# Making the next tile's input over six steps of the second part, with its product on GpSimd

## The chip, the cores and the metric

The kernel runs on one core of a Trainium2 chip. The metric is the device time of one execution in microseconds (us); the time before is the median of 3 runs. A TensorE matmul needs its weights loaded first (PEld in the profile), and the load of the next weights runs beside the matmul before it.

## The reference

Two things follow each other. First a long convolution by Fourier transforms, multiplied by the input; then a feed-forward layer on the result:

```python
h_filt = (np.maximum(pos_emb @ w1, 0.0) @ w2) * window      # 12480 x 128
u = x * v                                                   # 2 x 12480 x 128
y = irfft(rfft(u, 2 * S) * rfft(h_filt, 2 * S))[:, :S, :]
a = (x * y).reshape(24960, 128)
h = a @ w_in                                                # 128 -> 2048
return (h * (1.0 / (1.0 + np.exp(-h)))) @ w_out             # 2048 -> 128
```

All arrays are float32.

## The kernel before

The transform is written as matmuls in stages (98 x 64 points), with the spectrum in pairs of frequencies. The program has a first part, in which the filter and the transform of batch 0 are made, and a second part, the loop over `steps` (L886), which is the feed-forward layer with the transform of batch 1 beside it.

The second part goes over 52 token tiles of up to 490 columns (tokens), and in each over 16 blocks f of 128 hidden values; one (tile n, block f) is a step s. A tile's input is a pair ah, al: the high part of a = x * y, rounded to the type that TensorE takes, and the rest. A step does

- three matmuls into hq, a PSUM tile with three buffers: high weights with ah (L893), high weights with al (L894), low weights with ah (L895);
- Silu on ScalarE (L900), into hq itself while work of batch 1 is left (`beside`), otherwise into the SBUF tile g with two buffers;
- the rounding of the result to gh, on VectorE (L902), or on ScalarE (L904) when f is a multiple of 4 (of 5 once nothing is beside);
- the low part gl on VectorE (L905), which reads the Silu result and gh;
- three matmuls of the step three before (LAG) into op (L921 to L923), the output's sum.

Every engine takes its instructions in the order in which they stand in the program. There are no other priorities. Between the steps `batch1_steps` (a generator, L777) puts the work of batch 1, spread evenly over the first 384 steps: first groups of stage A (product x * v on GpSimd L269, matmuls L238, copies L244), then, for each of 49 pairs of frequencies, loads of tables (L315) and of the filter's spectrum (L795) on SP's queue, roundings on ScalarE (L803), low parts on GpSimd (L809), matmuls L441, products and sums on VectorE and GpSimd (L466, L473, L479, L483), and a store.

The input of the next tile is made by `attn_tile` (L668), all of it behind step f = 8 (L907): 80 small matmuls into yp (L677), a copy of half of yp to s2 on ScalarE (L688), the sum and the difference on VectorE (L691, L692, and for some tiles one column more, L699), the product with x on VectorE (L702), the rounding to ah on ScalarE (L703), the rest al on VectorE (L704). For tile 0 the same function is called ahead of the loop (letter Y of the hand-written order `seq3`, L746). The data for the tile after the next come by `load_tile` (L656) behind step f = 9: two requests on SP's queue, one for the transform's output of all tokens of the tile (L660), one for x (L665). Each has one buffer, so the first waits until the matmuls L677 have read it and the second until L702 has.

Of the kernel before, what the change touches and what calls it, by code (L numbers as in the profile page):

```python
# [14 lines left out]
ALU = mybir.AluOpType  # L15
# [44 lines left out]
def tile_offsets():  # L60
    offs, o = [], 0
    for b, i, t2, n in token_tiles():
        offs.append(o)
        o += sum(tile_widths(i, n))
    return offs, o
# [21 lines left out]
def kernel(  # L87
# [17 lines left out]
    nc = tc.nc  # L105
    ctx.enter_context(tc.manual_schedule())

    def pool(name, **kw):
        kw.setdefault("bufs", 1)
        return tc.alloc_tile_pool(name=name, reuse_waits="tile", **kw)  # L110
# [273 lines left out]
    for t in P["seq"]:  # L384
# [21 lines left out]
        elif t == "p":  # L406
            g = len(pts)
            pts.append(ppool.tile([128, NP, R], F32, name=f"pt{g}", tag="pt", bufs=8))
            for o in range(0, NP, 4) if g == 0 else [0]:
                n = 4 if g == 0 else NP  # L410
# [141 lines left out]
    def pair_u0(q):  # L552
        up = pp.tile([128, 2, NI, D], F32, name=f"up0_{q}", tag="up", bufs=2)
        for c in range(2):
            for k in range(2):
                nc.tensor.matmul(  # L556
                    up[64 * k : 64 * k + 64, c].rearrange("p i d -> p (i d)"),
                    fbs[q][:, 0, k, 64 * c : 64 * c + 64],
                    X[:, 2 * q + k],
                    start=True,  # L560
                    stop=True,
                )
        us = rp.tile([128, 2, NI, D], F32, name=f"us{q}", tag="uw", bufs=2)
        nc.scalar.copy(out=us, in_=up)  # L564
        return up, us
# [55 lines left out]
    pp = pool("pp2", space=PSUM)  # L621
# [3 lines left out]
    for it in range(-1, NQ):  # L625
        if it + 4 < NQ:
            fbs[it + 4] = load_fb(rpa, it + 4, 8, nc.sync if it < 0 else nc.scalar, fc)
        if it >= 0:
            up, us = pair_u0(it)
# [6 lines left out]
        if it >= 0:  # L636
            hab = habs.pop(it)
            at = products(it, up, hab[:, 1:2], "at", 4, nc.vector)
# [14 lines left out]
    tiles = token_tiles()  # L653
    offs, _ = tile_offsets()
# [13 lines left out]
    def attn_tile(n, wt, xs, psp, tag):  # L668
        b, i, t2, m = tiles[n]
        ws = tile_widths(i, m)  # L670
        w = sum(ws)

        yp = psp.tile([128, 2, 256], F32, name=f"yp{n}", tag=tag[0], bufs=tag[1])
        for t in range(m):
            for c in range(2):
                for h in range(0, D, 32):
                    nc.tensor.matmul(  # L677
                        yp[h : h + 32, c, t * HT : (t + 1) * HT],
                        wt[:, c, t * D + h : t * D + h + 32],
                        fai_sb[:, c],  # L680
                        start=True,
                        stop=True,
                    )
        at = mt.tile([128, 490], F32, name=f"att{n}", tag="att", bufs=1)
        ah = mt.tile([128, 512], F32R, name=f"ah{n}", tag="ah", bufs=2)
        al = mt.tile([128, 512], F32R, name=f"al{n}", tag="al", bufs=2)
        s2 = mt.tile([128, 256], F32, name=f"s2{n}", tag="s2", bufs=1)
        nc.scalar.copy(out=s2[:, 0 : m * HT], in_=yp[:, 1, 0 : m * HT])  # L688
        y1, y2 = (a[:, 0 : m * HT].rearrange("p (t j) -> p t j", t=m) for a in (yp[:, 0], s2))
        o, r = m * HT, ws[0] - HT  # L690
        nc.vector.tensor_tensor(out=at[:, 0:o].rearrange("p (t j) -> p t j", t=m), in0=y1, in1=y2, op=ALU.add)  # L691
        nc.vector.tensor_tensor(  # L692
            out=at[:, o : o + m * r].rearrange("p (t j) -> p t j", t=m),
            in0=y1[:, :, 1 : 1 + r],
            in1=y2[:, :, 1 : 1 + r],
            op=ALU.subtract,
        )
        if w > o + m * r:
            nc.vector.tensor_tensor(  # L699
                out=at[:, w - 1 : w], in0=y1[:, m - 1, HT - 2 : HT - 1], in1=y2[:, m - 1, HT - 2 : HT - 1], op=ALU.subtract  # L700
            )
        nc.vector.tensor_tensor(out=at[:, 0:w], in0=at[:, 0:w], in1=xs[:, 0:w], op=ALU.mult)  # L702
        nc.scalar.copy(out=ah[:, 0:w], in_=at[:, 0:w])  # L703
        nc.vector.tensor_tensor(out=al[:, 0:w], in0=at[:, 0:w], in1=ah[:, 0:w].bitcast(F32), op=ALU.subtract)  # L704
        return ah, al

    ahead, attn = {}, {}
    n_a = n_t = n_h = n_l = 0
    n_r = 4
    for t in P["seq3"]:  # L710
        if t == "x":
            uv.load()
        elif t in "md":
            uv.mul(nc.vector if t == "d" else nc.gpsimd)
        elif t in "Aa":
            stage_a_group(1, n_a, psa, uss.pop(n_a), 2, t == "A")
            n_a += 1
        elif t == "s":
            pair_s(*prods[NQ - 1])
        elif t == "v":  # L720
            pair_v(prods[NQ - 1][0], nc.vector)
        elif t == "u":
            last_w(NQ - 2)
        elif t == "U":
            last_w(NQ - 1)
            rp.release()
            rpa.release()
            mw = pool("mw")
            wo_split[:] = (mw.tile([128, NF * D], F32R, name=f"wo{k}") for k in "hl")
            mt = pool("mt")  # L730
        elif t == "S":
            nc.scalar.activation(out=warm_sb, in_=w2_sb[0:1, 0:1], func=AF.Silu)
        elif t == "L":
            ahead[n_t] = load_tile(n_t)
            n_t += 1
        elif t == "r":
            load_raw(n_r, spare[:, (n_r - 4) // 2 * 2, 256 * (n_r % 2) : 256 * (n_r % 2) + 256], wod)
            n_r += 1
        elif t == "h":
            split_hi(n_h, wo_split)  # L740
            n_h += 1
        elif t == "l":
            split_lo(n_l, wo_split)
            n_l += 1
        elif t == "Y":
            attn[0] = attn_tile(0, *ahead.pop(0), pp, ("up", 2))  # L746
    NA = n_a
    woh, wol = wo_split
    wih, wil = wi_split
# [7 lines left out]
    pmy = pool("pmy", space=PSUM)  # L757
# [4 lines left out]
    class Carved:  # L762


        at = dict(hab=(0,), at=(1024,), bt=(1792,), uw=(2560,), ws=(3072,), fb=(3584, 5868))
# [119 lines left out]
    op = {}  # L885
    for s in range(len(steps) + LAG):  # L886
        if s < len(steps):
            n, f = steps[s]
            w = sum(tile_widths(*tiles[n][1::2]))
            ah, al = attn[n]  # L890
            hp = pm.tile([128, 512], F32, name=f"hq{s}", tag="hq", bufs=3)
            fs = slice(f * 128, (f + 1) * 128)
            nc.tensor.matmul(hp[:, 0:w], wih[:, fs], ah[:, 0:w], start=True, stop=False)  # L893
            nc.tensor.matmul(hp[:, 0:w], wih[:, fs], al[:, 0:w], start=False, stop=False)  # L894
            nc.tensor.matmul(hp[:, 0:w], wil[:, fs], ah[:, 0:w], start=False, stop=True)  # L895
            beside = done < total
            g = hp if beside else moe.tile([128, 490], F32, name=f"g{s}", tag="g", bufs=2)
            gh = moe.tile([128, 512], F32R, name=f"gh{s}", tag="gh", bufs=P['lag'] + 1)
            gl = moe.tile([128, 512], F32R, name=f"gl{s}", tag="gl", bufs=P['lag'] + 1)
            nc.scalar.activation(out=g[:, 0:w], in_=hp[:, 0:w], func=AF.Silu)  # L900
            if f % P['fp'] if beside else f % P['fg']:
                nc.vector.tensor_copy(gh[:, 0:w], g[:, 0:w])  # L902
            else:
                nc.scalar.copy(out=gh[:, 0:w], in_=g[:, 0:w])  # L904
            nc.vector.tensor_tensor(out=gl[:, 0:w], in0=g[:, 0:w], in1=gh[:, 0:w].bitcast(F32), op=ALU.subtract)  # L905
            gs[s] = gh, gl
            if f == 8 and n + 1 < len(tiles):  # L907
                attn[n + 1] = attn_tile(n + 1, *ahead.pop(n + 1), pmy, ("yp", 1))
            if f == 9 and n + 2 < len(tiles):
                ahead[n + 2] = load_tile(n + 2)  # L910
            while done < total and done * n_side < (s + 1) * total:
                done += next(side, total)
        if s >= LAG:
            n, f = steps[s - LAG]
            w = sum(tile_widths(*tiles[n][1::2]))
            if f == 0:
                op[n] = pm.tile([128, 512], F32, name=f"op{n}", tag="op", bufs=2)
            o = op[n]
            fs = slice(f * 128, (f + 1) * 128)
            gh, gl = gs.pop(s - LAG)  # L920
            nc.tensor.matmul(o[:, 0:w], woh[:, fs], gh[:, 0:w], start=(f == 0), stop=False)  # L921
            nc.tensor.matmul(o[:, 0:w], woh[:, fs], gl[:, 0:w], start=False, stop=False)  # L922
            nc.tensor.matmul(o[:, 0:w], wol[:, fs], gh[:, 0:w], start=False, stop=(f == NF - 1))  # L923
            if f == NF - 1:
                ot = moe.tile([128, 490], F32, name=f"ot{n}", tag="ot", bufs=2)
                nc.scalar.copy(out=ot[:, 0:w], in_=o[:, 0:w])
                nc.scalar.dma_start(out=out[:, offs[n] : offs[n] + w], in_=ot[:, 0:w])
                del op[n], attn[n]
# [98 lines left out]
```

## Time and profile before

| | us |
|---|---|
| median of 3 runs (1582.66 to 1583.68) | 1583.28 |
| the profiled execution | 1582.48 |
| its span, first to last instruction | 1580.7 |

| engine | busy, us | share of the span |
|---|---|---|
| TensorE matmuls | 1536.4 | 97% |
| TensorE weight loads | 1302.8 | 82% |
| VectorE | 1273.2 | 81% |
| ScalarE | 1029.0 | 65% |
| GpSimd | 547.9 | 35% |

The mean granted TensorE clock is 0.992. Durations in the profile overlap a little: an engine starts its next instruction before the last one's end, and the ends of matmuls are modelled. An idle time is put down to the instruction whose completion came last before it ended.

### The profile page before, as it was taken

To read this page: it belongs to the slowest core of one execution; us is meant where nothing else is said; L and a number is where in the kernel's file an instruction comes from. 1 tells how busy PE (TensorE), PEld (TensorE's weight loads), DVE (VectorE), ACT (ScalarE), POOL (GpSimd) and SP (SyncE) were. 2 spreads that over 40 slices of the span, in tenths; PEclk is the share of its full clock that TensorE was granted. 3 is DMA by queue.
4 is the path that set the end of the run, shared out by engine and by line. 5 is a ranking of instruction groups with operands and counts; after the bars stand their busy time and mean duration, and the time that the engine had idled before them with its cause. 6 is when DMAs were issued, how large, how long until landed. Compare 5 with 4: busy or idle time off the path is not lost.

```text
span 1580.7 us, 34674 instructions
## 1 busy us (share of the span) xinstructions
PE 1536.4 (97%) x13420; PEld 1302.8 (82%) x13420; DVE 1273.2 (81%) x2148; ACT 1029.0 (65%) x2022; POOL 547.9 (35%) x520
## 2 busy tenths in 40 slices
PE   8979999799999999999999999999999999999999
PEld 7966776688888888888888888888888898888888
DVE  7658998666699889999999998777777777777776
ACT  2446676677777778777778775555555555555555
POOL 2557777422266656666666650000000000000000
PEclk9989999899999999999999999999999999999999
DMA  8567787734245454544554431111111111111110
GB/s 248 185 201 214 245 267 235 219 100 140 79 128 144 125 146 135 151 133 137 139 145 138 133 113 54 48 48 52 33 47 50 48 45 39 45 52 50 34 44 16
DMA packets 135213, 182.12 MB, mean 115 GB/s; under 512 B 10357, under 2 KB 78521, under 8 KB 135049
## 3 DMA queue, kind: packets, MB, share of 16 engines
q1 hardware_dynamic: 94024, 140.18, 31.1%
q10 hardware_dynamic: 40384, 37.63, 7.7%
q8 instruction: 106, 1.74, 0.5%
q0 software_dynamic: 640, 2.10, 0.4%
q14 instruction: 59, 0.48, 0.1%
HBM read 126.44 MB, written 53.42 MB: 114 GB/s over the span
## 4 chain that ended last, share of the span: by engine, by line
PE 75%; DVE 9%; ACT 4%; issue 4%; DMA 3%; POOL 2%; SPq 1%; ACTq 0%; DVEq 0%; POOLq 0%
PE hq L893 10%; PE op L921 10%; PE hq L894 10%; PE hq L895 10%; PE op L923 10%; PE op L922 10%; PE yp L677 2%; PE ap L238 2%; PE wp L609 2%; PE up L556 2%; PE ap L211 2%; DVE gl L905 2%; PE sp L573 2%; PE up L441 1%; PE wp L441 1%
## 5 line engine op out<-in xcount | busy, mean ns | idle before, releaser
L900 ACT ACTIVATE g<-hq 128x486 f32<-128x486 f32 (+3 forms) x448 | 252.8, 570 | 195.5 <-PE hq L895 175.1
L905 DVE TENSOR_TENSOR gl<-g,gh 128x486 fp32r<-128x486 f32 (+3 forms) x448 | 292.1, 657 | 73.1 <-PE hq L895 38.3
L893 PE MATMUL hq<-ah,wih 128*128 128x490 f32 (+3 forms) x832 | 320.8, 386 | 5.9 <-DVE gl L905 5.6
L921 PE MATMUL op<-gh,woh 128*128 128x490 f32 (+3 forms) x832 | 323.6, 389 | 0.0
L894 PE MATMUL hq<-al,wih 128*128 128x490 f32 (+3 forms) x832 | 317.2, 381 | 0.2 <-DVE al L704 0.2
L895 PE MATMUL hq<-ah,wil 128*128 128x490 f32 (+3 forms) x832 | 317.1, 381 | 0.0
L923 PE MATMUL op<-gh,wol 128*128 128x490 f32 (+3 forms) x832 | 316.9, 381 | 0.0
L922 PE MATMUL op<-gl,woh 128*128 128x490 f32 (+3 forms) x832 | 315.1, 379 | 0.0
L905 DVE TENSOR_TENSOR gl<-hq,gh 128x490 fp32r<-128x490 f32 (+2 forms) x384 | 250.8, 661 | 26.4 <-ACT gh L904 16.2
L900 ACT ACTIVATE hq<-hq 128x490 f32<-128x490 f32 (+2 forms) x384 | 212.4, 558 | 74.3 <-PE hq L895 46.0
L902 DVE CAST gh<-hq 128x490 fp32r<-128x490 f32 (+2 forms) x288 | 188.7, 655 | 41.4 <-ACT hq L900 39.6
L893 PEld LDWEIGHTS hq<-ah,wih 128*128 128x128 f32 x832 | 156.6, 188 | 40.8 <-DVE gl L905 16.0
L894 PEld LDWEIGHTS hq<-al,wih 128*128 128x128 f32 x832 | 158.2, 190 | 25.4 <-DVE al L704 0.7
L895 PEld LDWEIGHTS hq<-ah,wil 128*128 128x128 f32 x832 | 157.2, 189 | 24.8
L923 PEld LDWEIGHTS op<-gh,wol 128*128 128x128 f32 x832 | 156.7, 188 | 25.4
L902 DVE CAST gh<-g 128x486 fp32r<-128x486 f32 (+3 forms) x336 | 137.3, 409 | 49.9 <-ACT g L900 43.6
L921 PEld LDWEIGHTS op<-gh,woh 128*128 128x128 f32 x832 | 156.3, 188 | 23.2
L922 PEld LDWEIGHTS op<-gl,woh 128*128 128x128 f32 x832 | 156.8, 188 | 21.6 <-DVE gl L905 0.3
L703 ACT CAST ah<-att 128x490 fp32r<-128x490 f32 (+3 forms) x52 | 30.9, 595 | 97.4 <-DVE att L702 97.4
L591 POOL TENSOR_TENSOR bt<-us,hab 128x512 f32<-128x512 f32 x49 | 67.7, 1382 | 50.9 <-ACT us L564 33.3
L466 POOL TENSOR_TENSOR slots<-slots 128x512 f32<-128x512 f32 x49 | 63.5, 1296 | 61.4 <-ACT slots L460 61.4
L479 DVE TENSOR_TENSOR at<-at,bt 128x768 f32<-128x768 f32 x49 | 72.7, 1485 | 13.5 <-POOL bt L597 13.5
(1068 smaller groups left out, 2415.2 us busy)
## 6 DMA issues: line engine op xcount, KB each, us to landing
slots<-hs SPq DMA_DIRECT2D x98, 256.0 KB
slots<-wd SPq DMA_DIRECT2D x48, 490.0 KB
hs<-hab SPq DMA_DIRECT2D x49, 256.0 KB
slots<-in_fb_dram SPq DMA_DIRECT2D x49, 256.0 KB
wd<-slots ACTq DMA_DIRECT2D x49, 256.0 KB
wd<-ws SPq DMA_DIRECT2D x23, 512.0 KB
fb<-in_fc_dram ACTq DMA_DIRECT2D x45, 256.0 KB
xs<-in_x_dram SPq DMA_DIRECT2D x32, 196.0 KB
```

The costliest lines, as they stand in the source:

```text
L466: e.tensor_tensor(out=t[:, 0:2].rearrange("p k (i d) -> p k i d", i=NI), in0=u, in1=hab[:, :, m, 0].unsqueeze(2).broadcast_to([128, 2, NI, ...
L479: nc.vector.tensor_tensor(out=at, in0=at, in1=bt, op=ALU.add)
L591: e.tensor_tensor(out=t[:, 0:2].rearrange("p c (i d) -> p c i d", i=NI), in0=u, in1=h0.unsqueeze(2).broadcast_to([128, 2, NI, D]), op=ALU. ...
L893: nc.tensor.matmul(hp[:, 0:w], wih[:, fs], ah[:, 0:w], start=True, stop=False)
L894: nc.tensor.matmul(hp[:, 0:w], wih[:, fs], al[:, 0:w], start=False, stop=False)
L895: nc.tensor.matmul(hp[:, 0:w], wil[:, fs], ah[:, 0:w], start=False, stop=True)
L900: nc.scalar.activation(out=g[:, 0:w], in_=hp[:, 0:w], func=AF.Silu)
L902: nc.vector.tensor_copy(gh[:, 0:w], g[:, 0:w])
L905: nc.vector.tensor_tensor(out=gl[:, 0:w], in0=g[:, 0:w], in1=gh[:, 0:w].bitcast(F32), op=ALU.subtract)
L921: nc.tensor.matmul(o[:, 0:w], woh[:, fs], gh[:, 0:w], start=(f == 0), stop=False)
L922: nc.tensor.matmul(o[:, 0:w], woh[:, fs], gl[:, 0:w], start=False, stop=False)
L923: nc.tensor.matmul(o[:, 0:w], wol[:, fs], gh[:, 0:w], start=False, stop=(f == NF - 1))
```

## The change

`attn_tile` becomes a generator with five yields. At f = 8 it is created and run to its first yield (the matmuls and the allocation of the tiles); at each of f = 9 to 13 its next segment is issued: the copy to s2; the sum and the difference; the product, now on GpSimd; the rounding to ah; the low part al. The load for tile n + 2 moves from f = 9 to f = 12. Tile 0's input is made in one go as before, with its product on GpSimd too.

```diff
         s2 = mt.tile([128, 256], F32, name=f"s2{n}", tag="s2", bufs=1)
+        attn[n] = ah, al
+        yield
         nc.scalar.copy(out=s2[:, 0 : m * HT], in_=yp[:, 1, 0 : m * HT])
...
+        yield
         nc.vector.tensor_tensor(out=at[:, 0:o].rearrange("p (t j) -> p t j", t=m), in0=y1, in1=y2, op=ALU.add)
...
-        nc.vector.tensor_tensor(out=at[:, 0:w], in0=at[:, 0:w], in1=xs[:, 0:w], op=ALU.mult)
+        yield
+        nc.gpsimd.tensor_tensor(out=at[:, 0:w], in0=at[:, 0:w], in1=xs[:, 0:w], op=ALU.mult)
+        yield
         nc.scalar.copy(out=ah[:, 0:w], in_=at[:, 0:w])
+        yield
         nc.vector.tensor_tensor(out=al[:, 0:w], in0=at[:, 0:w], in1=ah[:, 0:w].bitcast(F32), op=ALU.subtract)
-        return ah, al
...
-            attn[0] = attn_tile(0, *ahead.pop(0), pp, ("up", 2))
+            for _ in attn_tile(0, *ahead.pop(0), pp, ("up", 2)):
+                pass
...
             if f == 8 and n + 1 < len(tiles):
-                attn[n + 1] = attn_tile(n + 1, *ahead.pop(n + 1), pmy, ("yp", 1))
-            if f == 9 and n + 2 < len(tiles):
+                nxt = attn_tile(n + 1, *ahead.pop(n + 1), pmy, ("yp", 1))
+            if 8 <= f < 14 and n + 1 < len(tiles):
+                next(nxt, None)
+            if f == 12 and n + 2 < len(tiles):
                 ahead[n + 2] = load_tile(n + 2)
```

## Rows read from the trace of the kernel before

**Rows 1.** The page, part 1: busy us, share of the span, instructions.

```profile
PE 1536.4 (97%) x13420; PEld 1302.8 (82%) x13420; DVE 1273.2 (81%) x2148; ACT 1029.0 (65%) x2022; POOL 547.9 (35%) x520
```

**Rows 2.** Three windows of the second part: busy us (instructions), clock, DMA share, GB/s.

```profile
303.35:402.79 99.44, 96.61 (x688) 84.27 (x687) 63.36 (x103) 75.36 (x150) 29.87 (x24) 0.98 0.41 122
402.79:934.26 531.47, 525.08 (x4114) 449.31 (x4113) 478.00 (x795) 408.99 (x817) 325.75 (x339) 1.00 0.49 135
934.26:1580.70 646.44, 642.63 (x4999) 548.96 (x4997) 498.17 (x943) 373.46 (x673) 5.69 (x6) 1.00 0.15 44
```

**Rows 3.** Waits, 402.79 to 934.26 us: total us, times, longest us.

```profile
ACT ah L703 <- DVE att L702: 41.5, 20, 3.1
...
PEld hq L893 <- DVE gl L905: 16.0, 31, 1.3
...
DVE al L704 <- ACT ah L703: 13.3, 20, 0.7
```

**Rows 4.** Timeline, one tile's input (yp at 579.9): start us, us, instruction, [idle before].

```profile
582.57 0.67 DVE L702 TENSOR_TENSOR att<-att,slots 128x490 f32<-128x490 f32 x1
...
583.27 0.60 ACT L703 CAST ah<-att 128x490 fp32r<-128x490 f32 x1 [1.81 <-DVE att L702]
...
586.80 0.67 DVE L905 TENSOR_TENSOR gl<-hq,gh 128x490 fp32r<-128x490 f32 x1
...
587.52 0.19 PEld L893 LDWEIGHTS hq<-ah,wih 128*128 128x128 f32 x1 [1.34 <-DVE gl L905]
...
587.86 0.39 PE L894 MATMUL hq<-al,wih 128*128 128x490 f32 x1
```

**Rows 5.** Timeline, one of the first three tiles, ScalarE and TensorE.

```profile
356.28 0.60 ACT L703 CAST ah<-att 128x490 fp32r<-128x490 f32 x1 [1.81 <-DVE att L702]
...
358.84 1.57 PE L238 MATMUL ap<-fa_sb,slots 98*128 98x196 f32 x8 [0.62 <-issue]
```

**Rows 6.** Lines, GpSimd's products: count, busy us, mean ns, idle us before them.

```profile
L466 POOL TENSOR_TENSOR slots<-slots 128x512 f32<-128x512 f32 x49 | 63.5, 1296 | 61.4 <-ACT slots L460 61.4
...
L473 POOL TENSOR_TENSOR slots<-slots 128x256 f32<-128x256 f32 x49 | 36.3, 742 | 0.0
```

**Rows 7.** Timeline, the first weight load of the second part.

```profile
303.35 0.28 PEld L893 LDWEIGHTS hq<-ah,wih 128*128 128x128 f32 x1 [0.24 <-ACT ah L703]
```

**Rows 8.** Timeline in the second half, matmuls, ScalarE and VectorE around one tile's input.

```profile
1088.79 0.58 ACT L900 ACTIVATE g<-hq 128x490 f32<-128x490 f32 x1 [0.76 <-PE hq L895]
...
1090.04 0.67 DVE L905 TENSOR_TENSOR gl<-g,gh 128x490 fp32r<-128x490 f32 x1 [0.85 <-PE hq L895]
...
1101.89 0.67 DVE L905 TENSOR_TENSOR gl<-g,gh 128x490 fp32r<-128x490 f32 x1
...
1103.23 0.67 DVE L702 TENSOR_TENSOR att<-att,slots 128x490 f32<-128x490 f32 x1
...
1104.25 0.38 PE L895 MATMUL hq<-ah,wil 128*128 128x490 f32 x1
...
1107.43 0.67 DVE L905 TENSOR_TENSOR gl<-g,gh 128x490 fp32r<-128x490 f32 x1
...
1108.46 0.67 DVE L905 TENSOR_TENSOR gl<-g,gh 128x490 fp32r<-128x490 f32 x1
...
1112.04 0.39 PE L894 MATMUL hq<-al,wih 128*128 128x490 f32 x1
```

**Rows 9.** Timeline in the first part, GpSimd's and VectorE's instructions on SBUF operands.

```profile
199.60 1.27 POOL L591 TENSOR_TENSOR bt<-us,hab 128x512 f32<-128x512 f32 x1
...
199.62 2.07 DVE L479 TENSOR_TENSOR at<-at,bt 128x768 f32<-128x768 f32 x1 [0.62 <-POOL bt L597]
...
202.87 0.95 DVE L479 TENSOR_TENSOR at<-at,bt 128x768 f32<-128x768 f32 x1
...
211.65 0.92 POOL L597 TENSOR_TENSOR bt<-us,hab 128x256 f32<-128x256 f32 x1
...
211.91 0.95 DVE L512 TENSOR_TENSOR wil<-spare,wih 128x256 fp32r<-128x256 f32 x1
```

## The prediction

> **What bounds the kernel now.** I read the shares of the engines first: TensorE is busy 97% of the span [rows 1], so a gain can only come out of the places where it stands still, and a loss out of a new such place. Next come the windows by stage [rows 2]. The second part of the program (52 tiles of 16 steps) begins at 303.35 us. Until 402.79 it runs beside the end of batch 1's first stage, until 934.26 beside batch 1's pairs (both "the first half" below), then alone ("the second half"). The reader is to see that VectorE is at 478.0 of 531.5 us in the middle window, 90%, while GpSimd is at 61% there and all but idle afterwards. TensorE's busy figures hide short stalls, so the third view is who waited for whom in the middle window [rows 3]: TensorE's weight load of a step's first matmul, L893, stood 16.0 us in 31 waits for VectorE's low part, L905. In that stretch a step's PSUM buffer hq (three of them) is only free when L905 of three steps before has read it.
>
> Fourth, one such place in order of time [rows 4]. Matmul yp of the next tile has run at 579.9. VectorE does the sum, the difference and the product L702, then stands for ScalarE's ah (13.3 us in 20 waits [rows 3]), then does al (L704). The low part of the step behind them starts only at 586.80, and the weight load that needs it at 587.52, after 1.34 us idle. ScalarE had itself stood 1.81 us for L702. So one burst on two engines, once a tile, is what TensorE pays for. In the second half the waits of TensorE are gone: a tile is 22.6 us of matmuls end to end, and the change can only lose there.
>
> The profiled execution took 1582.48 us (span 1580.7); the median of the runs is 1583.28, 0.8 higher. Terms below are differences from the profile, and are taken off the median.
>
> **The change part by part.** The generator adds no instruction. The same work for tile n+1, all issued behind step 8 before, is issued behind step 8 (matmuls), 9 (copy s2), 10 (sum, difference), 11 (product), 12 (ah) and 13 (al). It is needed at step 16, the next tile's first.
>
> 1. *The burst goes.* Lost time per wait is less than the idle time shown: in [rows 4] the load idled 1.34 up to 587.52. Loads of 0.19 us come every 0.22 when nothing is late, so this one was due at 586.21, its matmul at 586.43 and the next, L894, at 586.66. That one ran at 587.86, 1.20 late, so 0.14 of each wait is no loss. 31 waits: 16.0 - 31 x 0.14 = 11.7 us. **-11.7** if nothing new comes.
>
> 2. *In the first three tiles* the same wait of ScalarE (1.81 us) delays the copies of stage A's output, and TensorE stands 0.62 us at L238 [rows 5]. At 3 tiles about **-2.0**.
>
> 3. *The product moves.* VectorE loses 0.67 us a tile [rows 4]. GpSimd took 1296 ns for 512 columns and 742 for 256 of the same operation [rows 6], 2.16 ns a column, so 490 columns are 1.25 us (estimate). For the very first tile, which is still made in one go ahead of the loop, this lies on the path: TensorE waits for ah at 303.35 [rows 7]. 1.25 - 0.67 = **+0.6**.
>
> 4. *The product in GpSimd's queue, first half.* Behind it stand the pairs' low parts and products; ahead of it at most two operations of up to 1.3 us. GpSimd is busy 61% [rows 2] and an operation in progress has about 0.6 us left, so the product waits 0.4 us on average. ScalarE reaches ah two steps after the sum, behind Silu and, at step 12, a rounding as well; I reckon some 0.7 us of margin before al is late for step 16. One tile in four overruns, by about 0.6 us: 20 x 0.25 x 0.6 = **+3**. Bounds: 0, and 11.7 (the stall only moves to steps 13 to 16). I take a value near the lower end because GpSimd stands idle 39% of that stretch.
>
> 5. *The second half.* Here Silu's result lies in SBUF, so VectorE's L905 reads two SBUF operands, and that meets GpSimd. [Rows 9] show it: the add L479, 0.95 us alone, lasts 2.07 when it is issued 0.02 after a GpSimd product, and ends 0.82 after that product's end; so it stands until GpSimd is through. They take turns: L597 of GpSimd (211.65) gets in between two such adds of VectorE, and the second, issued at 211.91, takes 0.95 us for 256 columns. I follow one tile on its clock [rows 8]. Step 10's last hq matmul ends at 1104.63, Silu starts 0.04 later, and the low part 1.25 after Silu, as in another step whose rounding is on ScalarE (1088.79 to 1090.04): 1105.92. Low part, sum and difference take 1.34 (1101.89 to 1103.23): done at 1107.2. Product 1107.3 to 1108.55. L905 of step 11 stands behind it and ends at 1108.55 + 0.67 - 0.13 = 1109.1. Two more pairs of rounding and low part at 1.03 (1107.43 to 1108.46) and al start at 1111.1, end 1111.8; with 0.15 for the weight load 1111.9. The matmul that needs al, step 16's second, ran at 1112.04. So it just fits: 0 a tile, or up to 0.2 where the odd column's extra subtraction (0.15) comes in. 27 tiles x 0 to 0.15: **+2**.
>
> By the Trainium skill (SBUF - State Buffer, "Who interferes with whom") a cast can also run in a mode that holds the port shared with GpSimd; the cast L902 of step 11 would then hold the product up by some 0.2 us, and the term of the second half would be 4 instead of 2. No run here shows that, since GpSimd never worked beside that cast.
>
> 6. *The load of tile n+2* moves from step 9 to step 12 on SP's queue, both requests. 490 and 243 KB at the stretch's 135 GB/s [rows 2] are 5.4 us; due is the first at the next step 8, twelve steps of at least 1.33 us on. 0. The second request now waits for GpSimd's product instead of L702, and the pairs' loads of later steps queue behind it; loads of steps 9 to 11 now go ahead of it. 0, with up to 1 us in a few tiles if it fails; it is inside term 4's bounds. The buffers yp, s2 and att are held two to five steps longer and are free ten steps before their next use: 0.
>
> 7. *s2 a step later* finds its matmuls done; same length: 0.
>
> Sum: -11.7 - 2.0 + 0.6 + 3 + 2 = -8.1. 1583.3 - 8.1 = **1575.2 us**, 0.5% faster. Terms 1 to 3 alone give -13.1 (1570.2).
>
> **The rivals.** *Slower: al is late in every tile of the second half.* Place: the chain of term 5, which has 0.1 us to spare. If GpSimd gets the port only after L905 of step 11 as well, the product starts 0.7 us later, ScalarE's ah and Silu of step 13 with it, and al ends near 1112.5: 0.6 to 0.8 a tile, 27 tiles, +16 to +22. With -10.1 from the other terms that is 1589 to 1595. It decides from (10.1 + 3.2) / 27 = 0.49 us a tile. For it: VectorE is loaded without a break behind step 10, and TensorE has no slack. Against it: the turns taken in [rows 9].
>
> *No change: the stall moves.* Instead of VectorE's burst, ScalarE stands at ah for GpSimd, as it stood for L702 (41.5 us in 20 waits [rows 3]), Silu of step 13 comes late and step 16 pays; or the second half costs 0.3 a tile. Term 4 at 8 or term 5 at 8 brings the sum to about -2: 1581.5 us. For it: GpSimd is in order and its operations themselves wait for ScalarE. Against: GpSimd's slack.
>
> *The change doesn't do what it says* is excluded by the code: the operations are the same and every segment is run by step 13.
>
> **How the numbers follow.** Forecast (sum between -13 and -3.2) 0.62; no change 0.20; slower 0.18. About 0.2%, 3.2 us, is what a measurement can tell from none. The range leaves out little below (all of terms 1 and 2, nothing given back, 1569) and the worse half of the slower case above (1589).
>
> **What would show it.** Right: L893's waits for L905 fall from 16.0 us to under 5; ScalarE's wait at ah is for GpSimd and below 1 us a tile; in the second half one L905 a tile lasts 1.2 us or more, and tiles there stay within 0.2 of 22.6 us. Wrong: a wait of L894 for al in most tiles of the second half (the slower rival), or L893's waits as long as before, only later in the tile (no change).

## The result and the profile after

The changed kernel took **1604.64 us** (median of 4 runs, 1602.20 to 1607.72) beside 1582.97 for the kernel before on the same chip: a ratio of 1.0142, 95% interval 1.0127 to 1.0157. It is slower by some 22 us; the forecast was 1575.2, with a range that ended at 1589. The profiled execution took 1604.58 us, its span is 1602.7. Lines behind the edit have other numbers than before: L706 is the product, L708 ah, L710 al, L809 the pairs' roundings, L815 their low parts, L899 to L901 the hq matmuls, L906 Silu, L911 the low part gl.

First the page's part 1, against [rows 1]:

```profile
PE 1546.1 (96%) x13420; PEld 1301.8 (81%) x13420; DVE 1266.4 (79%) x2096; ACT 1033.2 (64%) x2022; POOL 623.5 (39%) x572
```

The 52 products have gone from VectorE to GpSimd, as the instruction counts say (2148 to 2096, 520 to 572). Then the same three stretches as in [rows 2]. Their cuts are the first weight loads of steps 0, 48 and 368, that is, of tiles 0, 3 and 23:

```profile
301.62:405.91 104.29, 97.87 (x687) 85.34 (x688) 61.00 (x98) 75.66 (x150) 34.32 (x27) 0.97 0.37 115
405.91:954.11 548.20, 531.52 (x4114) 449.35 (x4112) 476.81 (x775) 412.21 (x816) 361.59 (x359) 1.00 0.47 129
954.11:1602.70 648.59, 644.42 (x4999) 546.94 (x4997) 494.92 (x917) 374.42 (x674) 42.11 (x35) 1.00 0.16 45
```

The second part begins 1.73 us earlier, the first three tiles are 4.85 us longer (99.44 before), the middle stretch 16.73 (531.47 before), the second half 2.15 (646.44 before). So the loss lies where the transform of batch 1 runs beside. The cuts are not quite the ends of batch 1's stages, as the prediction takes them: in the kernel before, the first stage's last matmuls L238 end at 421.08 us and the pairs' last L441 at 949.90, so the second half begins with one more tile beside the pairs. Waits in the middle stretch (total us, times, longest), of GpSimd, TensorE's weight loads and ScalarE:

```profile
POOL att L706 <- DVE att L695: 25.4, 8, 4.2
POOL att L706 <- DVE att L702: 24.2, 10, 4.5
POOL att L706 <- ACT hq L906: 20.0, 1, 20.0
PEld hq L899 <- DVE gl L911: 11.3, 28, 1.1
...
PEld hq L900 <- DVE al L710: 8.7, 10, 1.4
...
ACT ah L708 <- POOL att L706: 2.6, 5, 1.0
...
PEld up L441 <- POOL xs15l L815: 1.6, 1, 1.6
...
PEld up L441 <- POOL xs25l L815: 1.5, 1, 1.5
```

Three readings. ScalarE's stand at ah is gone (2.6 us in 5, against 41.5 in 20 [rows 3]), as intended. But GpSimd now stands at the product for VectorE's difference: the idle times in front of the 20 products of this stretch, the one of 20.0 left out, have a mean of 2.7 us. (That one lies ahead of the pairs' first matmuls.) And TensorE waits for what was hardly ever late before: al, and the pairs' low parts on GpSimd (L441). One tile shows how these hang together (timeline of after, the step that issues the product and those behind it; start us, us, instruction, [idle before]):

```profile
693.07 0.62 ACT L809 CAST xs25h<-X 128x512 fp32r<-128x512 f32 x1
...
698.40 0.15 DVE L702 TENSOR_TENSOR att<-yp,s 128x1 f32<-128x1 f32 x1
...
698.62 1.89 POOL L706 TENSOR_TENSOR att<-att,slots 128x486 f32<-128x486 f32 x1 [4.48 <-DVE att L702]
...
700.47 1.30 POOL L815 TENSOR_TENSOR xs25l<-X,xs25h 128x512 fp32r<-128x512 f32 x1
...
701.83 0.19 PEld L441 LDWEIGHTS up<-xs25l,fw25h 128*128 128x128 f32 x1 [1.49 <-POOL xs25l L815]
...
702.40 0.75 POOL L483 TENSOR_TENSOR slots<-slots 128x256 f32<-128x256 f32 x1
...
703.18 0.62 ACT L809 CAST vs24h<-slots 128x512 fp32r<-128x512 f32 x1 [2.03 <-POOL slots L483]
...
703.71 0.56 ACT L906 ACTIVATE hq<-hq 128x486 f32<-128x486 f32 x1
...
704.30 0.66 DVE L908 CAST gh<-hq 128x486 fp32r<-128x486 f32 x1 [3.04 <-ACT hq L906]
...
705.55 1.28 POOL L466 TENSOR_TENSOR slots<-slots 128x512 f32<-128x512 f32 x1 [0.38 <-ACT slots L460]
705.58 1.78 DVE L710 TENSOR_TENSOR al<-att,ah 128x486 fp32r<-128x486 f32 x1
...
707.41 0.19 PEld L900 LDWEIGHTS hq<-al,wih 128*128 128x128 f32 x1 [1.05 <-DVE al L710]
```

The rounded xs25h was ready at 693.69. Its low part stood behind the product in GpSimd's queue until 700.47, nearly seven microseconds, and GpSimd did nothing for 4.48 of them. TensorE paid 1.49. The rest of the row comes late in turn: L483 on GpSimd, for which ScalarE stood 2.03 at the rounding vs24h, with Silu behind it, for which VectorE stood 3.04; then al, which TensorE waited for again.

In the first three tiles the product stands ahead of stage A's product x * v (L269) in the same way (timeline of after; the idle time is put down to L244, but VectorE's difference L695 had ended only at 361.96):

```profile
361.56 0.40 DVE L695 TENSOR_TENSOR att<-yp,s 128x240 f32<-128x240 f32 x1
...
362.10 1.23 POOL L706 TENSOR_TENSOR att<-att,slots 128x490 f32<-128x490 f32 x1 [15.90 <-ACT X L244]
...
363.28 2.49 POOL L269 TENSOR_TENSOR slots<-slots 98x512 f32<-98x512 f32 x2
...
364.61 1.59 PE L238 MATMUL ap<-fa_sb,slots 98*128 98x196 f32 x8 [1.89 <-POOL slots L269]
```

### The profile page after: what moved, and what is told of

Its sections match the earlier page's. It is cut to its first block, busy times and chain, and to the rows that moved or that the text cites. A ratio compares the mean times of both kernels' runs of the same rounds, so it can differ in the third digit from the quotient of the medians.

```text
span 1602.7 us, 34725 instructions
## 1 busy us (share of the span) xinstructions
PE 1546.1 (96%) x13420; PEld 1301.8 (81%) x13420; DVE 1266.4 (79%) x2096; ACT 1033.2 (64%) x2022; POOL 623.5 (39%) x572
## 4 chain that ended last, share of the span: by engine, by line
PE 55%; issue 5%; POOL 5%; DVE 4%; ACT 3%; DMA 0%; ACTq 0%; POOLq 0%; SPq 0%; DVEq 0%
PE op L929 9%; PE hq L900 9%; PE hq L899 8%; PE hq L901 8%; PE op L931 8%; PE op L930 8%; PE yp L677 2%; PE up L441 1%; DVE gl L911 1%; PE wp L441 1%; DVE al L710 1%; POOL slots L466 1%; DVE gh L908 1%; ACT hq L906 1%; POOL slots L483 1%
## 5 line engine op out<-in xcount | busy, mean ns | idle before, releaser
L906 ACT ACTIVATE g<-hq 128x486 f32<-128x486 f32 (+3 forms) x448 | 255.8, 571 | 233.3 <-PE hq L901 177.5
L911 DVE TENSOR_TENSOR gl<-g,gh 128x486 fp32r<-128x486 f32 (+3 forms) x448 | 316.6, 711 | 76.9 <-PE hq L901 41.6
L706 POOL TENSOR_TENSOR att<-att,slots 128x490 f32<-128x490 f32 (+3 forms) x52 | 66.9, 1287 | 699.2 <-DVE att L695 345.8
L899 PE MATMUL hq<-ah,wih 128*128 128x490 f32 (+3 forms) x832 | 321.4, 386 | 4.9 <-DVE gl L911 3.5
L900 PE MATMUL hq<-al,wih 128*128 128x490 f32 (+3 forms) x832 | 319.4, 384 | 6.5 <-DVE al L710 6.4
L901 PE MATMUL hq<-ah,wil 128*128 128x490 f32 (+3 forms) x832 | 316.9, 381 | 0.0
L906 ACT ACTIVATE hq<-hq 128x490 f32<-128x490 f32 (+2 forms) x384 | 213.5, 558 | 105.4 <-PE hq L901 79.5
L911 DVE TENSOR_TENSOR gl<-hq,gh 128x490 fp32r<-128x490 f32 (+2 forms) x384 | 250.6, 661 | 27.7 <-ACT gh L910 17.6
L908 DVE CAST gh<-hq 128x490 fp32r<-128x490 f32 (+2 forms) x288 | 189.0, 656 | 75.7 <-ACT hq L906 74.5
L908 DVE CAST gh<-g 128x486 fp32r<-128x486 f32 (+3 forms) x336 | 136.5, 406 | 69.2 <-ACT g L906 67.7
L900 PEld LDWEIGHTS hq<-al,wih 128*128 128x128 f32 x832 | 158.2, 190 | 38.9 <-DVE al L710 13.4
L899 PEld LDWEIGHTS hq<-ah,wih 128*128 128x128 f32 x832 | 156.8, 188 | 40.4 <-DVE gl L911 11.9
L901 PEld LDWEIGHTS hq<-ah,wil 128*128 128x128 f32 x832 | 157.4, 189 | 23.8
L479 DVE TENSOR_TENSOR at<-at,bt 128x768 f32<-128x768 f32 x49 | 72.8, 1485 | 13.5 <-POOL bt L597 13.5
L466 POOL TENSOR_TENSOR slots<-slots 128x512 f32<-128x512 f32 x49 | 63.5, 1297 | 45.7 <-ACT slots L460 40.1
```

The lines of the kernel that those rows point to most:

```text
L466: e.tensor_tensor(out=t[:, 0:2].rearrange("p k (i d) -> p k i d", i=NI), in0=u, in1=hab[:, :, m, 0].unsqueeze(2).broadcast_to([128, 2, NI, ...
L479: nc.vector.tensor_tensor(out=at, in0=at, in1=bt, op=ALU.add)
```

## The experiments

In the expectations Q is the theory that GpSimd's queue behind the product costs the time; S, that the spread itself puts the tile's input too late; D, that the later load does; L, that al comes too late for the next tile; W, that the spread costs wherever it stands. The text under each says which range was met. "The change" is the kernel after. Ratios are to the kernel before, run on the same chip. An added or dropped yield shifts the line numbers behind it: the weight load of a step's first matmul is L899 in the change and L900 in e9_vector_gap. The table sums the waits of TensorE's weight loads from 300 to 960 us of each profile (the waits view, those at the matmuls L677 left out, which are 8 us in each kernel), as us / times. Less the 22.0 of before, the totals follow the measured differences (22.2 of 21.7 us for the change; the others within 7 us, but for e4_later, which lost in the second half as well), so the waits in these columns are most of the loss.

| kernel | ratio, 95% interval | gl | al | pairs (L441) | L238 | other | total |
|---|---|---|---|---|---|---|---|
| before | 1 | 16.0/31 | 0.7/1 | 0.9/2 | 4.2/4 | 0.2/1 | 22.0 |
| after | 1.0142 (1.0127 to 1.0157) | 11.5/29 | 9.5/11 | 11.0/16 | 7.7/4 | 4.5/7 | 44.2 |
| e1_vector | 1.0067 (1.0052 to 1.0083) | 13.8/38 | 13.4/21 | 0.7/2 | 2.0/2 | 6.0/11 | 35.9 |
| e2_burst_gpsimd | 1.0209 (1.0193 to 1.0225) | 26.9/29 | 0.8/1 | 12.4/12 | 6.0/4 | 2.5/1 | 48.6 |
| e3_split_load | 1.0171 (1.0150 to 1.0192) | 11.4/30 | 9.7/11 | 11.1/16 | 8.0/4 | 3.9/6 | 44.1 |
| e4_later | 1.0355 (1.0332 to 1.0377) | 0.5/2 | 36.6/22 | 2.5/5 | 0.5/1 | 0.8/1 | 40.9 |
| e5_early_vector | 0.9990 (0.9981 to 0.9999) | 17.5/25 | 1.1/1 | 0 | 1.1/1 | 1.2/1 | 20.9 |
| e6_early_gpsimd | 1.0122 (1.0105 to 1.0138) | 20.1/27 | 0.8/1 | 11.0/14 | 4.2/4 | 0.9/1 | 37.0 |
| e7_early_gap | 0.9959 (0.9947 to 0.9970) | 6.8/22 | 0.8/1 | 1.5/4 | 4.1/4 | 2.6/1 | 15.8 |
| e8_from8_vector | 1.0015 (1.0004 to 1.0026) | 22.9/41 | 0.7/1 | 0.9/2 | 1.1/1 | 0.4/1 | 26.0 |
| e9_vector_gap | 0.9940 (0.9925 to 0.9955) | 7.5/23 | 1.2/1 | 0 | 1.1/1 | 2.9/1 | 12.7 |
| e10_two_gaps | 0.9974 (0.9959 to 0.9988) | 4.7/14 | 0.8/1 | 4.7/6 | 1.1/1 | 0 | 11.3 |
| e11_change_gap | 1.0002 (0.9993 to 1.0011) | 6.3/19 | 7.8/11 | 2.1/4 | 4.3/4 | 1.8/3 | 22.3 |
| e12_al_late | 0.9957 (0.9941 to 0.9973) | 7.9/23 | 6.6/10 | 0 | 0.7/1 | 3.1/1 | 18.3 |

**The product back on VectorE** (e1_vector), in the changed kernel:

```diff
-        nc.gpsimd.tensor_tensor(out=at[:, 0:w], in0=at[:, 0:w], in1=xs[:, 0:w], op=ALU.mult)
+        nc.vector.tensor_tensor(out=at[:, 0:w], in0=at[:, 0:w], in1=xs[:, 0:w], op=ALU.mult)
```

> The changed kernel with the product put back on VectorE; the six steps and the load at step 12 stay. Theory Q (GpSimd takes its work in order and stands at the product for VectorE's difference, 2.8 us a tile, with the pairs' low parts queued behind it): the first half's 22 us go and the burst's stalls go too, 1568 to 1576 us, and TensorE's waits for L815 at L441 vanish. Rival S (ah and al at steps 12 and 13 are too late for step 16, wherever the product is): 1595 to 1605, the waits of L900 for al stay near 13 us. Rival D (the load moved to step 12 holds up the pairs' loads on SP's queue): 1598 to 1607.

Measured: 1593.26 us, between the ranges of Q and S: about half of the loss is gone. The pairs' waits fall from 11.0 to 0.7 us, those at L238 from 7.7 to 2.0, so Q holds for these; al's do not fall (13.4 us), as S had it. Waits of e1_vector from 402 to 954 us:

```profile
ACT ah L708 <- DVE att L706: 18.9, 18, 1.9
...
PEld hq L899 <- DVE gl L911: 13.8, 38, 0.8
PEld hq L900 <- DVE al L710: 12.5, 20, 1.4
```

and one tile's end in its timeline:

```profile
746.40 0.60 ACT L708 CAST ah<-att 128x486 fp32r<-128x486 f32 x1 [1.08 <-DVE att L706]
...
747.42 0.56 ACT L906 ACTIVATE hq<-hq 128x486 f32<-128x486 f32 x1
...
749.26 1.27 POOL L466 TENSOR_TENSOR slots<-slots 128x512 f32<-128x512 f32 x1 [0.38 <-PE op L930]
749.29 1.77 DVE L710 TENSOR_TENSOR al<-att,ah 128x486 fp32r<-128x486 f32 x1
...
751.11 0.19 PEld L900 LDWEIGHTS hq<-al,wih 128*128 128x128 f32 x1 [1.44 <-DVE al L710]
```

Steps 9 to 13 are too late for al even without the product on GpSimd: ScalarE again stands at ah, now for VectorE's product, and Silu of a later step behind it. Both theories have a share.

**Only the product to GpSimd** (e2_burst_gpsimd): the kernel before, with its burst in one step, and the same line on GpSimd.

```diff
-        nc.vector.tensor_tensor(out=at[:, 0:w], in0=at[:, 0:w], in1=xs[:, 0:w], op=ALU.mult)
+        nc.gpsimd.tensor_tensor(out=at[:, 0:w], in0=at[:, 0:w], in1=xs[:, 0:w], op=ALU.mult)
```

> The kernel before with nothing changed but the product on GpSimd, in the burst behind step 8. Theory Q: GpSimd stands for the difference here too, and ScalarE and VectorE stand for the product in the burst: 1592 to 1610 us. Rival S: nothing is later but the product's own 0.6 us a tile, 1583 to 1590. Rival D: 1582 to 1586, as the load is where it was.

Measured: 1614.98 us beside 1581.45, 5 above Q's range and even more than after. Its waits from 402 to 954 us (lines of the kernel before):

```profile
ACT ah L703 <- POOL att L702: 51.2, 19, 3.7
...
PEld hq L893 <- DVE gl L905: 25.7, 28, 1.9
...
PEld up L441 <- POOL xs22l L809: 2.7, 1, 2.7
```

By the ratios the engine alone costs 33 us when product and input are issued together; the spread alone (e1) 11; both together 22. So the spread does heal part of what the engine costs, and the two shares do not add up.

**The first request of the load back at step 9** (e3_split_load; `load_tile` is split in two, and the second request, for x, stays at 12), for the theory that the later load costs something:

```diff
+            if f == 9 and n + 2 < len(tiles):
+                wt2 = load_tile(n + 2)
...
             if f == 12 and n + 2 < len(tiles):
-                ahead[n + 2] = load_tile(n + 2)
+                ahead[n + 2] = wt2, load_x(n + 2)
```

> The changed kernel with the load's larger request (L660) back at step 9 and only that for x (L665) at step 12. Theory Q and rival S: no difference, 1601 to 1608 us. Rival D: the part of the loss that the larger request makes comes back, 1585 to 1597; if it is the wait of the smaller one for the product, nothing changes here, but SP's waits at L665 would stand in front of late loads.

Measured: 1608.98 us, 1 above the range of Q and S and far from D's, with nearly the same waits as after in every column. So the place of the larger request costs nothing, as the prediction had it. The smaller one, which waits for the product, was not moved by itself.

**Product, ah, al and the load one step later** (e4_later), by one more yield ahead of the product:

```diff
+        yield
         yield
         nc.gpsimd.tensor_tensor(out=at[:, 0:w], in0=at[:, 0:w], in1=xs[:, 0:w], op=ALU.mult)
...
-            if 8 <= f < 14 and n + 1 < len(tiles):
+            if 8 <= f < 15 and n + 1 < len(tiles):
...
-            if f == 12 and n + 2 < len(tiles):
+            if f == 13 and n + 2 < len(tiles):
```

> The changed kernel with product, ah, al and load each one step later (12, 13, 14, 13). Theory Q: the difference is nearer to done when GpSimd comes to the product, so GpSimd stands some 1.5 us a tile less in the first half and the low parts are less late: 8 to 12 us less there, given back in part because al has one step less: 1592 to 1603 us in all. Rival S: al is later by a step in every tile, 1615 to 1640. Rival D: 1600 to 1610.

Measured: 1636.44 us, in S's range. The empty step between difference and product does its part (pairs 2.5 us, L238 0.5, gl 0.5), but al at step 14 is late in nearly every tile: 36.6 us in 22 here, and in the second half (waits view from 954 us on)

```profile
PEld hq L901 <- DVE al L711: 34.8, 29, 2.0
```

So step 14 is too late for al in both halves: one step's delay cost 34 us against after (2.13% by the ratios).

**All steps three earlier**, with the product on VectorE (e5_early_vector) and on GpSimd (e6_early_gpsimd). The edit of both, with e1's line too in e5:

```diff
-            if f == 8 and n + 1 < len(tiles):
+            if f == 5 and n + 1 < len(tiles):
...
-            if 8 <= f < 14 and n + 1 < len(tiles):
+            if 5 <= f < 11 and n + 1 < len(tiles):
...
-            if f == 12 and n + 2 < len(tiles):
+            if f == 9 and n + 2 < len(tiles):
```

> The six steps begin at step 5 instead of 8 (load at 9), product on VectorE: the same spread as in e1_vector, three steps earlier. Theory L (e1_vector loses because al, behind step 13's work in VectorE's queue, comes too late for step 16): the waits of L900 for al (15.4 us in 24) go and the stalls of TensorE at steps 0 to 2 (about 22 us) with them, the burst's stalls stay away: 1564 to 1574 us. Rival W (spreading itself costs, since ScalarE stands for the product at another place and Silu behind it is late wherever that is): the stalls move to steps 9 to 12, 1582 to 1595.

> As e5_early_vector, with the product on GpSimd (the change as it is, three steps earlier). Theory L with Q: the late al is gone, but GpSimd still stands at the product for VectorE's difference with the pairs' low parts behind it: TensorE's waits at L441 and L238 stay near 18 us, so 10 to 16 us above e5_early_vector, 1576 to 1590. If Q were wrong it would be within 3 us of e5_early_vector. Rival W: 1590 to 1605.

Measured: 1580.66 us for e5, between the ranges of L and W, and 1600.56 for e6, in W's range and 10 above that of L with Q. Starting earlier takes al's waits away in both (1.1 and 0.8 us). That is worth 12 us in e5 against e1, but only 3 in e6 against after, where gl's waits rise from 11.5 to 20.1. It does nothing for the pairs behind GpSimd's product (11.0 us in 14 in e6): that stall is one of order, not of lateness. The longest of them in e6:

```profile
PEld up L441 <- POOL xs22l L815: 2.0, 1, 2.0
```

In e5 a stall at gl is left, for the reason that bounded the kernel before: ScalarE stands at ah for the product. Waits of e5 from 402 to 954 us:

```profile
PEld hq L899 <- DVE gl L911: 17.0, 23, 1.8
ACT ah L708 <- DVE att L706: 16.7, 14, 1.9
```

**One empty step between difference and product** (e7_early_gap), in e6:

```diff
+        yield
         yield
         nc.gpsimd.tensor_tensor(out=at[:, 0:w], in0=at[:, 0:w], in1=xs[:, 0:w], op=ALU.mult)
```

(and the steps run to 11, the load stands at 10; so product, ah and al come a step later than in e6.)

> As e6_early_gpsimd, with one empty step between the difference and the product (matmuls at 5, s2 6, difference 7, product 9, ah 10, al 11, load 10). Theory Q: the difference is done when GpSimd comes to the product, nothing queues behind a standing product, and the waits at L441 and L238 fall to under 6 us: within 4 us of e5_early_vector, 1564 to 1577. Rival C (GpSimd's 1.25 us themselves are what the pairs lack): no better than e6_early_gpsimd.

Measured: 1575.32 us, in Q's range, against 1600.56 for e6: a gain of some 25 us by one empty step, and faster than before. The pairs' waits fall from 11.0 to 1.5 us, gl's from 20.1 to 6.8. The longest of the pairs' waits is now

```profile
PEld up L441 <- POOL fw2l L816: 0.5, 1, 0.5
```

The idle times in front of the product from 402 to 954 us, the longest left out, go from 2.5 to 0.8 us in the mean. So GpSimd's own time for the product, which is spent in both kernels, is not what the pairs lack (rival C).

**One step earlier only, on VectorE** (e8_from8_vector): e1 without the yield ahead of the copy to s2, so that al stands at step 12 (and the load at 11).

```diff
-        yield
         nc.scalar.copy(out=s2[:, 0 : m * HT], in_=yp[:, 1, 0 : m * HT])
```

> As e1_vector, with s2 behind step 8 with its matmuls and all that follows one step earlier (difference 9, product 10, ah 11, al 12, load 11). Theory L: one step more of room for al takes back most of the 22 us at steps 0 to 2: 1570 to 1580 us. Rival W: 1588 to 1596, as e1_vector.

Measured: 1585.14 us, between the ranges of L and W. One step takes al's waits from 13.4 to 0.7 us, but gl's rise to 22.9, so 8 of e1's 11 us are recovered.

**An empty step ahead of ah** (e9_vector_gap), in e5:

```diff
         nc.vector.tensor_tensor(out=at[:, 0:w], in0=at[:, 0:w], in1=xs[:, 0:w], op=ALU.mult)
+        yield
         yield
         nc.scalar.copy(out=ah[:, 0:w], in_=at[:, 0:w])
```

> As e5_early_vector (steps begin at 5, product on VectorE at 8), with one empty step between the product and ah (ah 10, al 11). What e5_early_vector still loses at steps 12 to 14 (13 us) is put down to ScalarE standing 16.7 us at ah for VectorE's product, with Silu behind it. If so: that wait falls under 4 us, the stalls at steps 12 to 14 go, 1565 to 1574 us. If those stalls come from the plain load of VectorE there, nothing changes: 1578 to 1583.

Measured: 1571.17 us, in the range, ratio 0.9940, the fastest of all: faster than the kernel before by 0.6% and than after by 2%. ScalarE no longer stands at ah, and gl's waits fall with it, from 17.5 to 7.5 us (waits from 402 to 954 us):

```profile
PEld hq L900 <- DVE gl L912: 7.5, 23, 0.7
...
ACT ah L709 <- DVE att L706: 1.1, 1, 1.1
```

**Both empty steps, product on GpSimd** (e10_two_gaps): e7 with one more yield ahead of ah, begun at step 4.

> As e7_early_gap, begun at step 4 and with an empty step before ah too (matmuls 4, s2 5, difference 6, product on GpSimd 8, ah 10, al 11, load 9). ScalarE hardly stood at ah any more in e7_early_gap (0.9 us in the first half), so the second gap should be worth little: 1572 to 1578 us. If al meets GpSimd's products less often at another step, some 3 us less.

Measured: 1575.59 us (1572.08 to 1581.09), in the range. It has the fewest waits of the table, but the profiled execution was its fastest run; by the ratios (0.9974 beside 0.9959, with intervals that overlap) it is no better than e7. What the other runs lost stays open.

**The change with only the copy and the difference moved** (e11_change_gap): copy to s2 at step 8, sum and difference at 9, step 10 empty; product, ah and al stay at 11, 12 and 13.

```diff
-        yield
         nc.scalar.copy(out=s2[:, 0 : m * HT], in_=yp[:, 1, 0 : m * HT])
...
+        yield
         yield
         nc.gpsimd.tensor_tensor(out=at[:, 0:w], in0=at[:, 0:w], in1=xs[:, 0:w], op=ALU.mult)
```

> The change with one edit: s2 behind step 8 with the matmuls and the difference at step 9, so that step 10 is empty; the product stays on GpSimd at 11, ah at 12, al at 13. Theory Q (GpSimd stands for the difference, the pairs' low parts behind it): GpSimd's idle time before the product falls from 2.8 us a tile to under 0.8, TensorE's waits at L441 and L238 from 19 us to under 6, and what stays is the late al: 1584 to 1595 us. If the late al alone makes the loss and the queue's waits only hide behind it: 1600 to 1606.

Measured: 1581.57 us, ratio 1.0002: the whole loss is gone, and the time is below Q's range (1584 to 1595). Waits from 402 to 954 us:

```profile
POOL att L706 <- DVE att L694: 27.7, 6, 18.6
POOL att L706 <- DVE att L701: 15.2, 8, 6.8
...
PEld hq L900 <- DVE al L710: 6.9, 10, 1.4
...
PEld hq L899 <- DVE gl L911: 6.3, 19, 0.6
...
PEld up L441 <- POOL fw15l L815: 1.1, 1, 1.1
```

The product's place in GpSimd's queue is the same as in the change; its input is ready earlier. The idle times of 18.6 and 6.8 us lie ahead of the first pair's matmuls and behind the last's; the other 19 have a mean of 1.1 us, beside 2.7 in the change (the expectation was under 0.8). The pairs' waits fall from 11.0 to 2.1 us, gl's from 11.5 to 6.3, L238's from 7.7 to 4.3. What is left of the loss is al (7.8), and it eats the gain. The edit also moves the copy and the difference on ScalarE and VectorE. In e4 these stay and the product goes a step later instead, and there the pairs' waits, L238's and gl's fall as well (2.5, 0.5 and 0.5 us): what the two have in common is the step between difference and product.

**e9 with al alone at step 13** (e12_al_late), by two yields ahead of al:

```diff
+        yield
+        yield
         yield
         nc.vector.tensor_tensor(out=al[:, 0:w], in0=at[:, 0:w], in1=ah[:, 0:w].bitcast(F32), op=ALU.subtract)
```

> As e9_vector_gap, with al alone two steps later (step 13, where the change has it; hq's product with al's weights stays where it is in the last step's neighbourhood, and ah stays at step 10). Theory A, al's place itself costs (at step 13 it stands behind that step's work in VectorE's queue and meets GpSimd's products, and the matmul that needs it follows at once): TensorE's waits for al come back as in e1_vector (15 us there) and the time is 1578 to 1590 us. Theory B, al was late in the change only because GpSimd and ScalarE ran late ahead of it: waits for al stay under 4 us, and the time is 1569 to 1574 us.

Measured: 1574.93 us, 0.9 above theory B's range and 3 below A's; by the ratios 2.7 us more than e9, with intervals that overlap a little. al's waits come back to 6.6 us in 10, half of e1's. So al's place at step 13 costs some 3 us by itself, as far as these intervals tell. The other half of its waits in e1 (13.4) came from what ran late ahead of it. Set beside e12's 6.6, most of al's waits in the change (9.5) and in e11 (7.8) go with its place.

## Why the prediction was wrong

*Term 4, the product in GpSimd's queue, is the step that failed.* It said +3 (0 to 11.7), and the middle stretch grew by 16.7 us and the three tiles ahead of it by 4.9, though the burst's stall was taken out of them. The term asked how long the product waits for GpSimd, and how late ah then is. It did not ask how long GpSimd waits for the product. It named what is queued behind ("the pairs' low parts and products") and gave that no price; it took a value near the lower end because GpSimd is idle 39% of the stretch. But in 18 of the 20 tiles GpSimd came to the product before VectorE had made the difference. Its idle time turned into a stand in front of work that was due. The Trainium skill states the order (Perfetto Trace Analysis, "Tensor Engine Instruction (MATMUL, LD_WEIGHTS)": ScalarE, VectorE and GpSimd are strict first-in, first-out), and the trace agrees: xs25l, whose input was ready at 693.69, ran at 700.47, behind the product. The bounds missed it too: the upper one, 11.7, took the loss as the old stall moved, not as new waits on GpSimd's own outputs. e11 and e7 show the cause. In e11 the product stays where it was and its input comes one step earlier: 22 us come back. In e7 the product comes one step later behind the same input: 25 us against e6.

The sign that the prediction had asked for, L893's waits (now L899's) under 5 us, was missed as well: 11.5 us in 29, now mostly at the tile's last and first steps. The sign that ScalarE would stand at ah for GpSimd, below 1 us a tile, came true (2.6 us in the middle stretch), and the loss came all the same.

*The margin for al*, also in term 4, is the second step that failed. "Some 0.7 us of margin before al is late for step 16" was reckoned from no row; with the spread it was not there. e1 has no work of the tile's input on GpSimd and still waits 13.4 us for al; one step earlier (e8) that is 0.7, and one step later than in the change (e4) 36.6 us in 22 waits.

*Terms 1 and 2, the prize*, were right in kind and a little too big. TensorE's lost time at step 12 of the tiles, where the burst made it stand, is some 10 us before (from the distances of successive matmuls' starts, less that of matmuls without a wait); term 1 had 11.7. The best kernel, e9, gets 7.6 us in tiles 4 to 22 and 2.3 in the first four (126.6 for 128.9 us; term 2 said 2.0). In the change these four tiles took 134.2 us, and with the product on VectorE (e1) 127.3: the product ahead of L269 is the reason, again GpSimd's queue.

*Term 5, the second half, was right*, in its mechanism too. It said +2, the window grew by 2.15. One tile of after there:

```profile
1128.05 0.40 DVE L908 CAST gh<-g 128x490 fp32r<-128x490 f32 x1
...
1128.26 1.29 POOL L706 TENSOR_TENSOR att<-att,slots 128x490 f32<-128x490 f32 x1 [21.32 <-DVE att L695]
...
1128.48 1.60 DVE L911 TENSOR_TENSOR gl<-g,gh 128x490 fp32r<-128x490 f32 x1
...
1132.06 0.67 DVE L710 TENSOR_TENSOR al<-att,ah 128x490 fp32r<-128x490 f32 x1
...
1132.78 0.19 PEld L900 LDWEIGHTS hq<-al,wih 128*128 128x128 f32 x1
```

The low part issued 0.22 us into the product lasts until 0.53 behind its end, as [rows 9] had it, and al is done 0.05 before the weight load that needs it. The cast L908 did not hold the product up by the 0.2 us that the prediction had set beside term 5: the product was issued 0.21 us into it and took 1.29, against 1.25 reckoned. That GpSimd stood idle 21.32 us in front of this product did no harm: nothing stood behind it. As the prediction asked, one L911 lasts 1.2 us or more in 27 of the 28 tiles here. al was late in 13 of them (waits view from 954.11 us on):

```profile
PEld hq L900 <- DVE al L710: 3.9, 13, 0.8
```

Eleven are tiles with the odd column, 0.21 us each, where term 5 had up to 0.2; the other two, of 0.78, are made during the two short tiles of 388 and 392 columns. The slower rival had put its loss here, at 0.6 to 0.8 us in every tile, and was wrong about the place; "no change" was right that ScalarE's and GpSimd's lateness would be paid at the next tile's start, but saw no price above the old one. *Term 3* cannot be told apart: the second part began 1.7 us earlier, and between 299.45 and 304.35 us in the fourteen profiles. *Term 6* (the load) was right for the larger request, by e3; for the smaller one no run shows it alone.

## What to carry to other kernels

Each engine here took its instructions in order, so an operation moved to a mostly idle engine has to be issued after its input is done: an empty step between them was worth 22 to 25 us here. Before such a move, list what stands behind the operation on its new engine and when each of those is due; the engine's idle share (39% here) did not tell of it. Spread work needs slack at every hand-over and the last piece well ahead of its deadline: al two steps later, at 13, cost some 3 us, and at 14, with product and ah a step later too, 34 more than the change.

## What the runs showed of the hardware

al reads two SBUF operands, and in the first half the spread put it beside GpSimd's products; the prediction had looked for that in the second half alone. By shape, from 402 to 935 us before and then from 402 to 954 after (count, busy us, mean ns, idle before):

```profile
L704 DVE TENSOR_TENSOR al<-att,ah 128x486 fp32r<-128x486 f32 x11 | 7.3, 666 | 7.3 <-ACT ah L703 7.3
```

```profile
L710 DVE TENSOR_TENSOR al<-att,ah 128x486 fp32r<-128x486 f32 x11 | 12.9, 1171 | 0.0
```

It took 666 ns before and 1171 after; in the second half of after, beside an idle GpSimd, the same form took 658. In the tile of the first section, al was issued at 705.58, 0.03 us behind L466 on GpSimd, and ended at 707.36, 0.53 behind that product's end at 706.83. The Trainium skill says so (SBUF — State Buffer, "Who interferes with whom": a VectorE instruction with two SBUF inputs contends with a GpSimd instruction that reads SBUF), and the trace agrees. It goes the other way too: in the same tile the product on GpSimd, issued 0.16 us behind VectorE's add L479 (698.46, 0.95 us), took 1.89 us instead of 1.25. How much of al's lateness at step 13 is this hold and how much the work ahead of it on VectorE was not tried separately; in e9, at step 11, al of 486 columns still took 932 ns and was hardly late (1.2 us in one wait).
